# A linear-attention and mixer kernel: batch 0's v cast, its chain of small products, and the order of batch 1's q loads

## The chip, the cores and the metric

The kernel runs on one core of a Trainium2 chip. A core has TensorE (matrix products into PSUM, with a separate weight load ahead of each product), VectorE, ScalarE, GpSimd and SyncE, which run side by side and wait for each other on semaphores, and 16 DMA engines between HBM and the on-chip SBUF. The metric is the time of one execution on the device in microseconds (us), the median of several runs.

## The reference

Attention without softmax, followed by a mixer with a low-rank product along the sequence and a two-layer network along the channels. Eight batches, eight heads, 576 positions, 64 channels a head; all inputs and the output are float32.

```python
theta = np.pi / 2.0 * pos / S
def phi(x, c, s):
    r = np.maximum(x, 0.0)
    return np.concatenate([r * c, r * s], axis=-1)
q_p, k_p = phi(q, cos_w, sin_w), phi(k, cos_w, sin_w)
kv = np.einsum('bhsf,bhsd->bhfd', k_p, v)
z = np.sum(k_p, axis=2)
num = np.einsum('bhsf,bhfd->bhsd', q_p, kv)
den = np.einsum('bhsf,bhf->bhs', q_p, z)[..., None] + 1e-06
attn = num / den
# x = attn, the heads side by side: (batch, 576, 512)
xt = x.transpose(0, 2, 1)
h = xt @ U @ V
u = x + h.transpose(0, 2, 1)
ch = np.maximum(u @ w_ch1, 0.0) @ w_ch2
return u + ch
```

## The kernel before

**Tiling.** The 576 positions are cut in nines: a pair of partitions holds nine consecutive positions, the even partition five and the odd one four. So q, k and v of a batch lie in SBUF as [128 partitions, 8 heads, 5 chunks, 64], chunk 4 (the tail) filled on even partitions alone. `load_odd` (L77) and `load_even` (L71) bring 512 KB and 640 KB for a whole tensor. The staging tiles qst, kst and vst exist once, so a batch's loads wait until the batch before has been read from them.

**Stages of a batch.** Features: VectorE and ScalarE make max(x, 0) times cos and sin of q and k in bf16 (`q_prep`, `k_prep`, L289 and L287). The q features are transposed on TensorE (`qtr_mm`, L368; `qtr_unit`, L356) and copied to SBUF. `kv_unit` (L315) makes kv of four heads, and normally a 65th column of ones in v gives the sum z with it. The x products (q features by kv) are multiplied by the reciprocal of the denominator. A is x by U (`a_mm`, L436); then u transposed is built in PSUM from x (products with the identity, `open_mm`, L935) and A by V (`uTd_mm`, L529). `g1_main` (L541) multiplies by w1 and ScalarE applies relu into `hid`; the second layer follows (`g2_part`, `w_part`).

**Order.** The program is written out by hand. Each engine runs its instructions in the order in which the program names them, and a waiting instruction holds all behind it. SyncE issues the loads of q, k, v; GpSimd issues the loads of U, V, w1 (`w1_load`, four quarters, cast from f32 to bf16 on the way) and w2 (`w2_load`, four quarters). Both use the same 16 DMA engines through two queues. Later batches follow a plan by slots (`attention_plan`), which the change leaves alone.

**Batch 0 is special.** Nothing can hide its attention, so `first_chain` (L942) lays it out step by step. z is summed by products of k features with a column of ones (`z_mm`, L892) into the tile `xz`, a pair of PSUM banks that also takes the denominators and A's sums. Products with a tile of zeros (`keep_warm`, L195) fill TensorE's waits. v is cast by VectorE into `v_ext` (four chunks, 65 columns a head, `v_block`) and its tail by GpSimd into `v_tl` (`v_prep`). The denominators are made for heads 0 to 3 and 4 to 7 apart (`den_mm`, L900), each group with its own reciprocal, and VectorE normalises all ten x blocks (`xh_norm`, L920). Tags such as G3 (three PSUM banks), T1, OA, OB name the banks that a product takes.

**Around the chain.** After the features of k come: the tail of v on GpSimd, w1's four loads (the first between the two tail casts), `first_chain`, the loads of batch 1 in the order q odd, q even, k odd, k even, four of v; then a one-column copy into `mark` on GpSimd that waits for batch 1's v of heads 0 to 3, and w2's four loads behind it. The products with w1 begin with three half blocks of `g1_main`, between which the last two blocks of u transposed are closed (`uTd_close`). Batch 1's q features (`q_prep(1, ...)`, chunk 4 first) come next on VectorE and ScalarE, and their transposes, from slot 1 on, on TensorE. The first product with w2 is at slot 16. SyncE's next loads, batch 2's, stand behind a gate: a two-byte copy that waits for w2's second quarter.

Of the kernel before, what the change touches and what calls it, by code (L numbers as in the profile page):

```python
# [10 lines left out]
FP32 = mybir.dt.float32  # L11
# [6 lines left out]
def kernel(  # L18
# [111 lines left out]
    for h0 in (0, 4):  # L130
        load_odd(vst, v, 0, h0, h0 + 4)
        load_even(vst, v, 0, h0, h0 + 4)
    def load_uv():
        nc.gpsimd.dma_start(out=stV, in_=moe_V)
        nines_u = moe_U.rearrange("(m k) r -> m (k r)", k=9)
        nc.gpsimd.dma_start(
            out=stU[:, 0:4, :].rearrange("p c r -> p (c r)"),
            in_=bass.AP(
                tensor=nines_u.tensor, offset=nines_u.offset,
                ap=[[9 * R, TS], [5 * R, 2], [1, 4 * R]],  # L140
            ),
        )
        for lo in (0, TS):
            nc.gpsimd.dma_start(out=stU[lo : lo + TS, 4, :], in_=nines_u[:, 4 * R : 5 * R])
# [59 lines left out]
    mark = const.tile([TS, 1], FP32)  # L204
    mark2 = const.tile([1, 1], BF16)

    V_nat = const.tile([R, S], BF16)
# [69 lines left out]

    def v_block(b, h0, h1, c0, c1, eng):
        cast(
            eng,  # L280
            v_ext[b % 2][:, c0:c1, h0:h1, 0:D].rearrange("p c h d -> p h c d"),
            vst[:, h0:h1, c0:c1, :],
        )

    def scaled_relu(eng, o, i, w):
# [29 lines left out]
    def kv_unit(b, hg, tag, bufs, eng=None):  # L315
        if b not in kv_sb:
            kv_sb[b] = pool.tile([P, H, E], BF16, tag="kv", bufs=2, name="kv")
        acc = bank([P, 4, E], FP32, tag, bufs, "kv_ps")
        vx = v_ext[b % 2]
        for i in range(4):  # L320
            h = hg * 4 + i
            for c in range(5):
                nc.tensor.matmul(  # L323
                    out=acc[:, i, :],
                    lhsT=k_p[b][:, c, h, :] if c < 4 else k_tl[:, h, :],
                    rhs=v_tl[:, h, :] if c == 4 and b < 2 else vx[:, c, h, :],
                    start=(c == 0),
                    stop=(c == 4),
                )
        cast(eng or V_, kv_sb[b][:, hg * 4 : hg * 4 + 4, :], acc)  # L330

# [588 lines left out]
    def xh_norm(b, c, h0, rec, acc):  # L920
# [6 lines left out]
            in0=acc[rows],  # L927
            in1=rec[rows, c, :].unsqueeze(2).to_broadcast([P if c < 4 else TS, 4, D]),
            op=ALU.mult,
# [5 lines left out]
    def open_mm(b, d, t, cs):  # L935
        for c in cs:
# [3 lines left out]
            )  # L940

    def first_chain(b, xz, v_ps):  # L942
        z = xz[:, 0, 0:H]
        d = [
            xz[:, 0, H + 20 * i : H + 20 * i + 20].rearrange("p (c h) -> p c h", h=4)
            for i in range(2)
        ]
        rec = [pool.tile([P, 5, 4], FP32, tag="rec5", bufs=2, name="rec5") for _ in d]
        for h0 in (0, 4):
            v_block(b, h0, h0 + 4, 0, 4, V_)  # L950
        cast(V_, V_bf, v_ps.rearrange("r (c p) -> r c p", c=4))
        cast(A_, z_sb, z)
        kv_unit(b, 0, *T1, A_)
        den_mm(b, 0, 4, d[0])
        recip(rec[0], d[0])
        x0 = [xh_mm(b, c, 0, *t) for c, t in zip(ORD, (G3, G3, G3, OA, OB))]
        den_mm(b, 4, 8, d[1])
        kv_unit(b, 1, *T1, A_)
        for n in range(2):
            xh_norm(b, ORD[n], 0, rec[0], x0[n])  # L960
        recip(rec[1], d[1])
        for n in range(2, 5):
            xh_norm(b, ORD[n], 0, rec[0], x0[n])
        x1 = [xh_mm(b, c, 4, *t) for c, t in zip(ORD[0:4], (G3, G3, G3, OA))]
        for n in range(2):
            xh_norm(b, ORD[n], 4, rec[1], x1[n])
        uT_alloc(b)
# [4 lines left out]
        for n in range(2, 5):  # L972
            xh_norm(b, ORD[n], 4, rec[1], x1[n])
        for i, (tag, bufs) in enumerate((T1, OB, OA)):
# [162 lines left out]
```

## Time and profile before

| what | value |
|---|---|
| median of 3 runs | 299.06 us (298.85 to 299.60) |
| profiled execution | 298.44 us, span 296.7 us |
| granted TensorE clock over the span | 1.0 |
| VectorE, ScalarE, GpSimd busy | 183.8, 158.1, 73.4 us |
| HBM read and written | 36.86 MB, 9.44 MB |
| transposes of batch 0's q on TensorE | 8.9 to 12.0 us |
| first kv product of batch 0 | 15.83 us |
| second kv eviction on ScalarE | 19.01 us |
| first product with w1 | 22.70 us |
| first transposes of batch 1's q | 25.28 us |
| first product with w2 | 40.28 us |

The profile is of one execution. Its span runs from the first instruction to the last; the rest of the execution's time lies around it. A row of the timeline has a start, a duration, the engine, the line of the program and the tiles that are written and read, and in brackets how long the engine had been idle and what ended that. Matmul rows overlap: a product of 512 columns takes 379 ns and the next starts 216 ns later. Times in this document count from the start of the span.

### The profile page before, as it was taken

Reading aid. Unit: us, or ns where it says so; the run is one execution under the profiler, and the core shown is the slowest. Engines: PE = TensorE matmul, PEld = TensorE weight load, DVE = VectorE, ACT = ScalarE, POOL = GpSimd, SP = SyncE. Lnnn points to the kernel's source line nnn. Section 1 sums busy time; section 2 is a strip of 40 time slices with the busy share of each in tenths; the row PEclk is TensorE's granted clock in tenths of the full one; section 3 lists DMA queues with packets and bytes.
Section 4 is the critical chain, followed back from the end, with each engine's and each line's share of the span. In section 5 each row is a group of like instructions: output and inputs, shape, how many; then the busy total and the mean of one; then the engine's idle time right before and its main releaser. Section 6 shows DMA issues by size and latency. Waiting matters only on the chain.

```text
span 296.7 us, 7055 instructions
## 1 busy us (share of the span) xinstructions
PE 290.1 (98%) x2948; PEld 195.1 (66%) x2948; DVE 183.8 (62%) x359; ACT 158.1 (53%) x269; POOL 73.4 (25%) x113
## 2 busy tenths in 40 slices
PE   8999999999999999999999999999999999999994
PEld 6775455545987547854887547855887547845982
DVE  4898748887884668738734687538734586404341
ACT  2835561476693467745692457746692453067300
POOL 8340500050053305540051500540051101300130
PEclk9999999999999999999999999999999999999999
DMA  7999999999949994999999808996375104030004
GB/s 205 352 273 255 226 186 261 291 232 236 287 82 164 266 357 106 251 241 269 232 163 226 325 2 198 177 310 187 73 129 171 38 2 88 8 136 2 0 15 165
DMA packets 85281, 53.30 MB, mean 180 GB/s; under 512 B 54018, under 2 KB 82978, under 8 KB 85250
## 3 DMA queue, kind: packets, MB, share of 16 engines
q1 hardware_dynamic: 78802, 41.40, 59.0%
q0 software_dynamic: 6368, 11.43, 15.6%
q8 instruction: 23, 0.38, 0.5%
q14 instruction: 8, 0.07, 0.1%
q10 hardware_dynamic: 80, 0.03, 0.0%
HBM read 36.86 MB, written 9.44 MB: 156 GB/s over the span
## 4 chain that ended last, share of the span: by engine, by line
PE 95%; DMA 2%; ACT 1%; DVE 0%; issue 0%; ACTq 0%
PE g_ps L551 38%; PE w_ps L729 29%; PE gt_ps L571 5%; PE o_ps L611 5%; PE ot_ps L638 5%; PE x_ps L413 3%; PE kv_ps L339 2%; DMA qst<-in_q_dram 2%; PE w_ps L198 1%; PE va_ps L464 1%; PE a_ps L439 1%; PE kv_ps L323 1%; PE t_ps L368 1%; PE t_ps L356 1%; PE xh_ps L914 1%; PE va_ps L484 0%
## 5 line engine op out<-in xcount | busy, mean ns | idle before, releaser
L560 ACT ACTIVATE hid<-g_ps 128x512 bf16<-128x512 f32 x128 | 76.1, 597 | 85.1 <-PE g_ps L551 58.4
L551 PE MATMUL g_ps<-uT,w_bf 128*128 128x512 bf16 x512 | 120.8, 379 | 0.0
L551 PEld LDWEIGHTS <-w_bf 128*128 128x128 bf16 x512 | 46.3, 98 | 48.8 <-issue 0.2
L741 POOL TENSOR_TENSOR o_sb<-w_sum,u_bf 128x512 f32<-128x512 f32 x21 | 26.4, 1283 | 124.0 <-DVE w_sum L741 124.0
L729 PEld LDWEIGHTS <-hid 128*128 128x128 bf16 x448 | 43.6, 98 | 5.6
L729 PEld LDWEIGHTS <-S 128*128 128x128 bf16 x336 | 32.6, 98 | 4.1 <-DVE S L697 0.2
L741 DVE TENSOR_TENSOR o_sb<-o_sb,w_ps 128x512 f32<-128x512 f32 x28 | 19.2, 686 | 17.5 <-PE w_ps L729 11.1
L729 PE MATMUL w_ps<-w_bf,hid 128*128 128x256 bf16 x224 | 26.9, 273 | 0.0
L729 PE MATMUL w_ps<-T,hid 128*128 128x256 bf16 x224 | 26.7, 273 | 0.0
L729 PE MATMUL w_ps<-T,S 128*128 128x256 bf16 x224 | 26.0, 273 | 0.0
L473 DVE TENSOR_TENSOR u_bf<-x_bf,va_ps 128x1024 bf16<-128x1024 bf16 x16 | 19.3, 1216 | 7.2 <-PE va_ps L464 7.2
L114 POOL CAST v_ext<-vst 128x512 bf16<-128x512 f32 (+1 forms) x30 | 19.3, 678 | 13.2 <-DMA vst<-in_v_dram 12.8
L423 DVE TENSOR_TENSOR x_bf<-x_ps,rec 128x512 bf16<-128x512 f32 x28 | 19.4, 691 | 1.0
L697 DVE TENSOR_TENSOR S<-hid 128x1024 bf16<-128x1024 bf16 x14 | 9.7, 693 | 15.3 <-ACT hid L560 15.3
L403 DVE TENSOR_SCALAR rec<-x_ps 128x8 f32<-128x8 f32 (+1 forms) x35 | 5.7, 164 | 20.1 <-PE x_ps L413 20.0
L287 ACT ACTIVATE k_p<-kst,sinw 128x512 bf16<-128x512 f32 x26 | 17.1, 712 | 0.2 <-DMA kst<-in_k_dram 0.2
L585 POOL DMA_DIRECT2D out_dram<-o_sb x12 | 7.6, 630 | 38.3 <-DVE o_sb L619 21.4
L114 DVE CAST kv<-kv_ps 128x520 bf16<-128x520 f32 (+1 forms) x8 | 5.1, 632 | 17.5 <-PE kv_ps L339 13.9
L611 PE MATMUL o_ps<-w_bf,hid 128*128 128x512 bf16 x64 | 15.6, 379 | 0.0
L571 PEld LDWEIGHTS <-w_bf 128*128 128x128 bf16 x256 | 14.7, 98 | 0.9
L571 PE MATMUL gt_ps<-uT_tl,w_bf 128*128 128x128 bf16 x256 | 15.3, 219 | 0.0
L638 PE MATMUL ot_ps<-w_bf,hid_tl 128*128 128x512 bf16 (+2 forms) x80 | 15.0, 336 | 0.0
(145 smaller groups left out, 366.2 us busy)
## 6 DMA issues: line engine op xcount, KB each, us to landing
qst<-in_q_dram SPq DMA_DIRECT2D x14, 512.0 KB, 6.2
kst<-in_k_dram SPq DMA_DIRECT2D x14, 512.0 KB, 9.1
vst<-in_v_dram SPq DMA_DIRECT2D x12, 512.0 KB, 8.2
out_dram<-o_sb POOLq DMA_DIRECT2D x12, 512.0 KB, 6.7
w_bf<-in_moe_w_ch_dram POOLq DMA_DIRECT2D x8, 512.0 KB, 10.6
out_dram<-o_sb SPq DMA_DIRECT2D x4, 512.0 KB, 3.0
qst<-in_q_dram SPq DMA_DIRECT2D x2, 640.0 KB, 7.0
kst<-in_k_dram SPq DMA_DIRECT2D x2, 640.0 KB, 10.8
```

The source lines that it names most:

```text
L114: eng.tensor_copy(out=o, in_=i)
L287: nc.scalar.activation(out=o, in_=i, func=AF.Relu, bias=0.0, scale=w)
L423: nc.vector.tensor_tensor(out=x_of(b, c, rows).rearrange("p (g i d) -> p g i d", g=2, d=D), in0=view[:, :, :, 0:D], in1=rec[rows].unsqueez ...
L473: nc.vector.tensor_tensor(out=u_bf[b][:, d0 : d0 + 2], in0=x_bf[b].rearrange("p c (d n) -> p d c n", n=P)[:, d0 : d0 + 2], in1=va_ps[b, d0 ...
L551: nc.tensor.matmul(out=g_ps.rearrange("p (c t) -> p c t", c=4), lhsT=w1_bf[:, d, j * P : j * P + P], rhs=uT[b][:, d, :, :], start=(d == 0) ...
L560: nc.scalar.activation(out=hid[b][:, j, :], in_=g_ps, func=AF.Relu, bias=0.0, scale=1.0)
L571: nc.tensor.matmul(out=g_ps[:, jj, :], lhsT=w1_bf[:, d, j * P : j * P + P], rhs=uT_tl[pr][:, d, :], start=(d == 0), stop=(d == 3),)
L611: nc.tensor.matmul(out=o, lhsT=hid[0][:, j, cc * P : cc * P + P], rhs=w2_bf[:, j, :], start=(j == 0), stop=(j == NJ - 1),)
L638: nc.tensor.matmul(out=o[:, cols], lhsT=hid_tl[pr][:, j, :], rhs=w2_bf[:, j, cols], start=(j == 0), stop=(j == NJ - 1),)
L697: V_.tensor_tensor(out=o, in0=a, in1=b_, op=op)
L729: nc.tensor.matmul(out=res[:, g, :], lhsT=lhs[:, k_, g * P : g * P + P], rhs=rhs[:, k_, :], start=(opens and k_ == 0 and g == 0), stop=(k_ ...
L741: eng.tensor_tensor(out=o, in0=x, in1=y, op=ALU.add)
```

## The change

Five things are done in the first 24 us and in the order around them.

- v of batch 0 is cast by VectorE alone, all five chunks, into a new tile `v0` in the space of `hid`, two heads, two heads and four heads at a time; kv of batch 0 has 64 columns a head. GpSimd's casts of the tail are gone.
- All denominators of batch 0 lie in one row, [5 chunks, 8 heads], with one reciprocal.
- The chain is dealt out anew: the sine of k's tail goes to VectorE; V_bf, one x block (`xh_norm_act`, four activations) and the second eviction of u transposed go to ScalarE; A's second half goes to VectorE, from a bank of its own. Banks and keep-warm products are moved, fills are added, and the spread of V comes ahead of k's last two z groups.
- GpSimd: w1's first load stands behind a one-column copy that waits for v of heads 0 to 3, the other three behind one that waits for ScalarE's first kv eviction.
- SyncE: between the odd and the even rows of batch 1's q stands a four-byte copy into `mark3` that waits for the last v of batch 0.

The three half blocks of `g1_main` follow the two closings together.

```diff
+    v0 = pool.tile([P, H, 5, D], BF16, tag="hid", bufs=1, name="v0")
...
+        n = D if b == 0 else E
+        acc = bank([P, 4, n], FP32, tag, bufs, "kv_ps")
...
+                    rhs=(
+                        v0[:, h, c, :] if b == 0
+                        else v_tl[:, h, :] if c == 4 and b < 2 else vx[:, c, h, :]
+                    ),
...
+    def xh_norm_act(b, c, h0, rec, acc):
+        x_alloc(b)
+        rows = slice(0, P) if c < 4 else tail(b)
+        for i in range(4):
+            nc.scalar.activation(
+                out=x_of(b, c, rows)[:, (h0 + i) * D : (h0 + i) * D + D],
+                in_=acc[rows, i, :], func=AF.Copy, bias=0.0,
+                scale=rec[rows, c, h0 + i : h0 + i + 1],
+            )
...
-        for h0 in (0, 4):
-            v_block(b, h0, h0 + 4, 0, 4, V_)
-        cast(V_, V_bf, v_ps.rearrange("r (c p) -> r c p", c=4))
-        cast(A_, z_sb, z)
-        kv_unit(b, 0, *T1, A_)
-        den_mm(b, 0, 4, d[0])
-        recip(rec[0], d[0])
+        d = xz[:, 0, H : H + 40].rearrange("p (c h) -> p c h", h=H)
+        rec = pool.tile([P, 5, H], FP32, tag="rec5", bufs=1, name="rec5")
+        fill(1)
+        for h in (0, 2):
+            cast(V_, v0[:, h : h + 2], vst[:, h : h + 2])
+        qtr_evac(b, 4, V_, t_q[4])
+        cast(V_, v0[:, 4:H], vst[:, 4:H])
+        cast(A_, z_sb, xz[:, 0, 0:H])
+        kv_unit(b, 0, *G3, A_)
+        cast(A_, V_bf, v_ps.rearrange("r (c p) -> r c p", c=4))
+        den_mm(b, 0, H, d)
+        recip(rec, d)
         x0 = [xh_mm(b, c, 0, *t) for c, t in zip(ORD, (G3, G3, G3, OA, OB))]
-        den_mm(b, 4, 8, d[1])
         kv_unit(b, 1, *T1, A_)
+        fill(2)
+        xh_norm_act(b, ORD[4], 0, rec, x0[4])
+        for n in range(4):
+            xh_norm(b, ORD[n], 0, rec, x0[n])
...
-        uTd_mm(b, 0)
-        uTd_evac(b, 0, A_)
-        uTd_mm(b, 1)
-        uTd_evac(b, 1, V_)
-        a_mm(b, a_ps, (2, 3), range(5))
-        cast(A_, A_of(b)[TS:P, :], a_ps[TS:P, :])
+        for i in range(2):
+            uTd_mm(b, i)
+            uTd_evac(b, i, A_)
+        a2 = bank([P, P], FP32, *G3, "a_ps")
+        a_mm(b, a2, (2, 3), range(5))
+        cast(V_, A_of(b)[TS:P, :], a2[TS:P, :])
...
-    keep_warm(2, *T1)
+    v_ps = None
     for c in TL:
-        k_prep(0, c, (V_, A_))
-        keep_warm(2 if c < 2 else 1, *T1)
+        k_prep(0, c, (V_, A_ if c < 4 else V_))
+        if c < 3:
+            keep_warm((3, 1, 1)[c], *T1)
+        if c == 3:
+            v_ps = spread_v(*T1)
         z_mm(0, c, xz[:, 0, 0:H])
-        if c == 1:
-            qtr_evac(0, 4, V_, t_q[4])
-    v_ps = spread_v(*OB)
     qtr_evac(0, 3, A_, t_q[3])
 
-    v_prep(0, 0, 4, (4,), (G_,))
+    G_.tensor_copy(out=mark, in_=vst[0:TS, 3, 4, 0:1])
     w1_load(0)
-    v_prep(0, 4, 8, (4,), (G_,))
+    first_chain(0, xz, v_ps)
+    G_.tensor_copy(out=mark[0:1], in_=kv_sb[0][0:1, 0, 0:1])
     for n in range(1, 4):
         w1_load(n)
-    first_chain(0, xz, v_ps)
     load_odd(qst, q, 1)
+    nc.sync.dma_start(out=mark3, in_=vst[0:1, 4, 4, 0:1])
     load_even(qst, q, 1)
...
-    g1_main(0, 0, True)
     uTd_close(0, 2, V_)
     uTd_close(0, 3, A_)
-    g1_main(0, 1, True)
-    g1_main(0, 2, True)
+    for j in range(3):
+        g1_main(0, j, True)
```

`fill(n)` makes n products of 384 columns with the tile of zeros into the second bank of `xz`.

More of the change, by code (lines that the diff above doesn't have):

```diff
@@ L205 @@
     mark2 = const.tile([1, 1], BF16)
+    mark3 = const.tile([1, 1], FP32)
     V_nat = const.tile([R, S], BF16)
@@ L317, in kv_unit @@
             kv_sb[b] = pool.tile([P, H, E], BF16, tag="kv", bufs=2, name="kv")
-        acc = bank([P, 4, E], FP32, tag, bufs, "kv_ps")
+        n = D if b == 0 else E
+        acc = bank([P, 4, n], FP32, tag, bufs, "kv_ps")
         vx = v_ext[b % 2]
@@ L329, in kv_unit @@
                 )
-        cast(eng or V_, kv_sb[b][:, hg * 4 : hg * 4 + 4, :], acc)
+        cast(eng or V_, kv_sb[b][:, hg * 4 : hg * 4 + 4, 0:n], acc)
     def kv_pair(b, tag, bufs):
@@ L927, in xh_norm @@
             in0=acc[rows],
-            in1=rec[rows, c, :].unsqueeze(2).to_broadcast([P if c < 4 else TS, 4, D]),
+            in1=rec[rows, c, h0 : h0 + 4].unsqueeze(2).to_broadcast([P if c < 4 else TS, 4, D]),
             op=ALU.mult,
@@ new lines, in first_chain, with fill @@
+    def first_chain(b, xz, v_ps):
+        def fill(n):
+            for _ in range(n):
+                nc.tensor.matmul(
+                    out=xz[:, 1, P:512], lhsT=zero[:, 0:P], rhs=zero[:, 0:384],
+                    start=True, stop=True,
+                )
+        d = xz[:, 0, H : H + 40].rearrange("p (c h) -> p c h", h=H)
[10 more added lines that the diff above has]
+        recip(rec, d)
@@ L956, in first_chain @@
         x0 = [xh_mm(b, c, 0, *t) for c, t in zip(ORD, (G3, G3, G3, OA, OB))]
-        den_mm(b, 4, 8, d[1])
         kv_unit(b, 1, *T1, A_)
-        for n in range(2):
[L960 to L966, printed above, removed]
+        fill(2)
@@ L967, in first_chain @@
+        xh_norm_act(b, ORD[4], 0, rec, x0[4])
+        for n in range(4):
+            xh_norm(b, ORD[n], 0, rec, x0[n])
+        x1 = [xh_mm(b, c, 4, *t) for c, t in zip(ORD[0:4], (G3, G3, G3, T1))]
+        for n in range(2):
+            xh_norm(b, ORD[n], 4, rec, x1[n])
         uT_alloc(b)
@@ L972, in first_chain @@
         for n in range(2, 5):
-            xh_norm(b, ORD[n], 4, rec[1], x1[n])
-        for i, (tag, bufs) in enumerate((T1, OB, OA)):
+            xh_norm(b, ORD[n], 4, rec, x1[n])
+        for i, (tag, bufs) in enumerate((OA, OB, T1)):
             uT_ps[b, i] = bank([P, 4, P], FP32, tag, bufs, "uT_ps")
```

13 lines of the change are left out of this document (removed).

## The prediction

> **What bounds the kernel now.** I read the page first: busy time and the 40 slices.
>
> ```profile
> PE 290.1 (98%) x2948; PEld 195.1 (66%) x2948; DVE 183.8 (62%) x359; ACT 158.1 (53%) x269; POOL 73.4 (25%) x113
> ...
> PE   8999999999999999999999999999999999999994
> ```
>
> TensorE is busy in every slice, so only its holes can be won, or new ones made. The second view, busy time by stretch, says where they are (columns: stretch, its length, busy us of PE, PEld, DVE, ACT, POOL, granted clock, DMA share, GB/s).
>
> ```profile
> 19.00:20.00 1.00, 0.55 (x16) 0.54 (x15) 1.00 (x4) 0.39 (x1) 0.00 (x0) 1.00 1.15 245
> ...
> 22.00:23.00 1.00, 0.74 (x10) 0.41 (x7) 0.26 (x1) 0.40 (x2) 0.00 (x0) 1.00 1.17 249
> ...
> 24.00:33.00 9.00, 9.00 (x79) 5.18 (x78) 8.04 (x16) 5.06 (x10) 0.00 (x0) 1.00 1.17 253
> ```
>
> After 24 us TensorE has no hole to speak of, at full clock; what can be gained lies ahead of that, and from 24 us on any operand that comes late is paid in full. The DMA engines are full throughout. Third, the chain of waits in order of time (start, us, what).
>
> ```profile
> 16.61 0.48 PE xz L903 x20
> 17.09 0.77 PE xh_ps L914 x20
> 17.86 0.48 PE xz L903 x20
> 18.34 0.66 PE kv_ps L323 x20
> 18.99 0.02 issue
> 19.01 0.40 ACT kv L112
> ...
> 22.16 0.28 ACT A_sb L112
> ...
> 22.48 0.38 PE u L937 x4
> ...
> 25.45 0.45 PE t_ps L356 x8
> ...
> 40.44 0.86 PE o_ps L611 x4
> ```
>
> The chain runs through TensorE with two breaks: the second kv eviction (19.01), and A_sb (22.16), which the fourth block of opening products waits for because it shares a bank with A's sums. At 25.28 by the timeline (25.45 in the chain) come the transposes of batch 1's q tail, at 40.28 the first products with w2. Fourth, the transfers, asked for by stretch: queue lines of 24 to 33, then of 42.1 to 46.0, then the issues at 11.00, 13.99 and 33.21 (last column: us from issue to landing).
>
> ```profile
> q0 software_dynamic: 1071, 1.06, 69.6%
> q1 hardware_dynamic: 1068, 1.20, 46.4%
> ...
> q0 software_dynamic: 792, 0.79, 123.0%
> ...
> qst<-in_q_dram SPq DMA_DIRECT2D x1, 640.0 KB, 7.7
> ...
> w_bf<-in_moe_w_ch_dram POOLq DMA_DIRECT2D x1, 512.0 KB, 8.4
> ...
> w_bf<-in_moe_w_ch_dram POOLq DMA_DIRECT2D x1, 512.0 KB, 5.7
> ```
>
> When both queues have work they share packet for packet (1071 to 1068 in 9 us), some 120 to 133 GB/s each as counted; alone, SyncE's queue moved 357 GB/s (13 to 15 us) and GpSimd's 208 (it casts, so it reads twice what is counted). From 42.1 to 46.0 SyncE's queue moved nothing, though the timeline has it issuing at 42.17, 43.05, 43.80 and 44.47: behind a full GpSimd queue a new transfer took 3.0 to 3.8 us to begin. At the start, with nothing else moving, it took 1.5 (issue 0.73, first packets 2.3).
>
> **The chain of batch 0, part by part.** TensorE from the end of the transposes, 12.00, to the first denominator product, 16.45: after the change four keep-warm products (4 x 0.22), a hole of 0.22 as before, five groups of z (0.22 each), two more keep-warm, the spread of V (0.39), one fill (0.16), 20 kv products (0.61): 3.8, to 15.76. That is 0.7 earlier. ScalarE allows it: its fourth sine product of k ends at 14.39 as before, the fourth z group wants it at 14.55, and k_tl's sine has gone to VectorE (0.40, starting 13.8).
>
> VectorE's casts of v start at 14.2. 640 contiguous columns are not in the trace: by the row of 512 (four casts in 1.42 us, 0.355 each) 0.44, by the row of 1024 (two in 1.68) 0.53. I take 0.5: two end by 15.2, and heads 2 and 3 want the second at 15.45. Cover 0.2; cost 0 to 0.1. The cast of four heads (0.9 to 1.05, after q_tlT's 0.6) ends by 16.9, wanted by the second kv unit at 17.5.
>
> Denominators: 40 products in one row (1.0) in place of 20 and 20 (0.5 each): nothing on the sum before the second kv unit, and one reciprocal pair less for VectorE (0.4). V_bf goes to ScalarE (0.60), which was idle from 17.03 to 19.01: hidden, and T's bank is free at 16.7, before the second kv unit. The two fills (0.33) lie in the hole at 18.8. The chunk that ScalarE normalises: four activations of 64 columns, between 0.16 (8 columns) and 0.27 (128 columns) each, 0.65 to 1.1 in all, ending 19.3 to 19.7; TensorE wants it at 19.45: 0 to 0.25, I take 0.1, which VectorE's four norms instead of five give back.
>
> A's second half now has a bank of its own and VectorE evicts it, so the fourth opening block no longer waits: the hole of 0.43 at 22.0 goes. Both uT evictions on ScalarE end at 21.9, when the first g products come. The halves of g1 start at 21.97 and end at 23.27; before, the same point was 24.41. **Gain 1.1**; 0.7 if the hole comes back at the closing products, 1.3 if the first hole goes too. GpSimd loses two casts (0.46, 0.62), off the path. w1's first quarter is issued at 13.7 instead of 13.99 and wanted at 22.0; at its old 8.4 it lands at 22.1, and with SyncE's queue empty beside it earlier: 0.
>
> **What moves in the queues.** On SyncE the small copy mark3 waits for batch 0's last v, issued at 6.22 and landed 8.8 later, 15.0. Behind it stand q's even rows (before: 11.00), k odd, k even and four v transfers. mark3 costs 0.76 like the copy at 42.17, so q even is issued at 15.9. w1's first quarter is in its queue by then, with packets from 16.3 (13.99 took until 16.6). So q even starts behind a running GpSimd queue: at best 1.5 later, 17.4; at worst 3.84, 19.7. I take 3.4, 19.3, because its neighbour says so: k odd, issued at 14.41, moved hardly anything before 18 (79 hardware packets against 246 software ones from 17 to 18.5). From there k odd, 512 KB, took until 23.5, 5.5 us; k even landed 4.5 after it. 640 KB shared: 5.8. **q even lands at 25.1** (23.2 to 25.5); before it was 18.7.
>
> Who waits: VectorE's cosine and ScalarE's sine of q_tl, which the new chain wants at 22.7, then TensorE's transposes of it, reached at 24.13. 25.1 and 0.87 (sine 0.71, hand-overs) make 25.97: **stall 1.84** (0 to 2.25). Chunks 0 to 3 follow at the old spacing.
>
> The Trainium skill's page "DMA: Bandwidth & Descriptors" (section "Latency and other measured facts") gives about 0.6 us to the first byte of a hardware-issued transfer. By it q even would start at 16.5 and land at 22.3, and there would be no stall; the rows above show 1.5 on an empty machine and 3.0 or more on a full one, so they decide, and the rule's result is the first rival.
>
> The same bytes with an idle gap in front (15.2, when q's odd rows are through, to 16.3) and SyncE's queue behind GpSimd's: batch 1's even v for heads 0 to 3, landed 33.0 before, comes at 34.8 to 35.6, and w2's four loads wait for it on GpSimd. 5.7 after issue w2's first quarter lands at 40.6 to 41.5; before it was 38.95. TensorE, shifted by -1.1 + 1.84 = +0.74, wants it at 41.0: 0 to 0.5, I take 0.25. Later things have cover: the last v, 1.2 late at 37.3, is cast by 39.4 and used at 41; batch 2's loads, behind w2's second quarter on SyncE, 1.7 late, feed ScalarE at 50.5 to 51.9, whose next product for TensorE is at 53.9. w1's other quarters, behind ScalarE's kv eviction on GpSimd (16.3 instead of 15.64), queue behind the first anyway.
>
> **Sum**, against the profiled execution's 298.44 (span 296.7 and 1.74 around it): 298.44 - 1.1 + 1.84 + 0.25 = 299.43, which is +1.0. The median of the runs is 299.06, 0.62 above that execution; on it 300.0.
>
> **Rivals.** First, the gate is harmless: q even starts at 17.4 or earlier, lands by 23.3, w2 by 39.2, and the chain's 1.1 stays: 298.0. For it: the idle start's 1.5 us, and one GpSimd transfer only just begun. Against it: k odd's slow beginning.
> Second, gain and stall cancel: start near 18.4, landing 24.2, stall 0.95, w2 in time: 298.9. For it: 18.4 lies between the two measured delays, 2.5 after the issue.
> Third, SyncE's queue is held until GpSimd's is drained, as 42.1 to 46.0 can be read too (w2's last load landed at 48.0): 2.1 MB of w1 at 208 GB/s from 16.3 end at 26.4, q even 2.8 later at 29.2 (0.66 MB at 357, and 1.0 to land), stall 5.9: 303.9. Against it: the even sharing from 18.5 on. It decides if no hardware packet is seen while w1 runs.
>
> **How the numbers follow.** About 0.3%, 0.9 us, is what a measurement of this kernel can tell from no change. Forecast, a stall that outweighs the gain: 0.42; gate harmless 0.24; cancelling 0.26; held 0.08. Slower is the first and last, 0.50; within 0.3% 0.26; faster 0.24. The range goes from the full gain at its upper bound, 297.8, to the smallest gain with the longest stall, -0.7 + 2.25 = +1.55 or 300.6, and 1.2 more for what lands late behind it (the lateness of the last v, if its cover fails): 301.8. The forecast's own range is 299.4 to 300.9.
>
> **What would show it.** Right: TensorE's first g products near 22.0, a hole of 1 to 2 us ahead of the q_tl transposes, VectorE and ScalarE there waiting for q's transfer, and a hole or none at 41 before the first w2 product. Wrong: q's even rows landed before 23.4; the first g products after 22.5; a hole at the second kv unit, which would mean that the casts of v are slow.

## The result, and the profile after

| what | before | after |
|---|---|---|
| median, 20 runs of each | 298.89 us (298.40 to 300.51) | 301.84 us (297.82 to 303.78) |
| ratio | | 1.0056, 95% interval 1.0029 to 1.0083 |
| profiled execution, span | 298.44, 296.7 us | 299.02, 297.1 us |
| first kv product of batch 0 | 15.83 | 14.64 |
| first product with w1 | 22.70 | 22.46 |
| first transposes of batch 1's q | 25.28 | 24.63 |
| first product with w2 | 40.28 | 41.00 |

The change makes the kernel slower, by 0.6% as the ratio has it. The ratio is one of means and leaves out the five runs of the changed kernel that lie over 1.5% above its fastest, so it is smaller than that of the two medians. The changed kernel's runs spread over 6 us, those of the kernel before over 2; the one that was profiled is among its shortest, and it shows only a part of what the change costs. The page of that execution (busy time, then the slices):

```profile
PE 289.1 (97%) x2916; PEld 195.7 (66%) x2947; DVE 183.3 (62%) x357; ACT 159.3 (54%) x273; POOL 72.7 (24%) x113
...
PE   8999989999999999999999999999999999999994
...
PEclk9979999999999999999999999999999999999999
```

The third digit of the last line is new: over the slice from 14.9 to 22.3 us the granted clock is 0.77 on average, because it is half from 16.49 to 19.90. The same stretches as before, in busy time by stretch (columns as there):

```profile
19.00:20.00 1.00, 1.00 (x24) 0.91 (x23) 0.77 (x3) 0.58 (x3) 0.00 (x0) 0.55 0.99 337
22.00:23.00 1.00, 1.00 (x9) 0.43 (x7) 0.44 (x1) 0.79 (x2) 0.00 (x0) 1.00 1.16 245
24.00:33.00 9.00, 8.95 (x78) 5.11 (x77) 7.30 (x14) 4.77 (x9) 0.00 (x0) 1.00 1.17 253
```

The holes of the first two stretches (0.55 and 0.74 us busy before) are gone, yet the clock in the first is 0.55: TensorE is busy there in part because its products take longer. In the third nothing is missing, so in this execution batch 1's q was not late. The chain of waits:

```profile
14.80 0.58 PE kv_ps L320 x20
15.38 0.99 PE xz L903 x40
...
18.00 16.50 DMA vst<-in_v_dram
...
34.62 0.18 POOL mark L1043
...
35.08 5.89 DMA w_bf<-in_moe_w_ch_dram
...
41.00 1.02 PE o_ps L611 x4
```

The 40 denominator products take the expected 1.0, kv comes a little over 1 us earlier, and what ends last is no longer TensorE: batch 1's v landed at 34.50 (33.03 before), the mark behind it let w2's first quarter start at 35.08, and that landed at 40.96, 2.0 later than before. TensorE stood 1.11 us for it. (A hole is counted here from the time at which the next product could have started, 216 ns after the start of the last; the idle times in the views count from that product's end and are 0.16 shorter.) The transfers by stretch: 16.17 to 17.62, 17.62 to 20.59 and 24 to 33, then the issue of q's even rows (15.11, last column: us to landing).

```profile
q0 software_dynamic: 287, 0.29, 122.4%
q1 hardware_dynamic: 2, 0.00, 0.3%
...
q1 hardware_dynamic: 693, 0.82, 87.9%
q0 software_dynamic: 68, 0.05, 11.7%
...
q0 software_dynamic: 1073, 1.07, 69.7%
q1 hardware_dynamic: 1074, 1.19, 46.2%
...
qst<-in_q_dram SPq DMA_DIRECT2D x1, 640.0 KB, 6.5
```

For 1.45 us SyncE's queue got nothing beside w1. Then, in this execution, w1's first quarter was through (19.05) and the second sent no packet before 20.59, so q's even rows had the engines almost alone and landed at 21.57. For q this is the rival that the prediction called harmless gate; for w2 it is not, since that rival had w2 by 39.2. Nor is it the usual course: in the four other profiles with mark3 q landed at 25.7 to 26.2.

Where every microsecond lies can be read from five times of a profile. The table gives, for each profiled execution of this study, the start of the first transposes of batch 0's q, then the us from there to the first w1 product, from there to the transposes of batch 1's q, from there to the first w2 product, and from there to the end (the execution's time less the sum of the others). In brackets are TensorE's holes above 0.5 us in that stretch that end with a transfer's landing, directly or by one operation behind it.

| kernel | first | to w1 | to q_tl | to w2 | rest | time |
|---|---|---|---|---|---|---|
| before | 8.89 | 13.81 | 2.58 | 15.00 | 258.16 | 298.44 |
| after | 8.62 | 13.84 | 2.17 | 16.37 (1.11) | 258.02 | 299.02 |
| e1_no_mark3 | 9.19 | 13.75 (1.05) | 2.17 | 14.99 | 258.10 | 298.20 |
| e2_warm | 8.28 | 13.46 | 5.36 (3.19) | 16.13 (1.13) | 258.01 | 301.24 |
| e3_before_mark3 | 8.83 | 13.80 | 4.31 (1.73) | 15.30 | 258.03 | 300.27 |
| e4_after_again | 8.45 | 13.20 | 5.27 (3.10) | 16.31 (1.30) | 258.05 | 301.28 |
| e5_no_mark3_warm | 8.26 | 15.24 (1.88) | 2.17 | 14.99 | 258.07 | 298.73 |
| e6_w1_after_k | 8.33 | 14.07 (0.62) | 2.17 | 15.02 | 258.08 | 297.67 |
| e7_before_less_warm | 8.43 | 15.62 | 2.37 | 14.99 | 258.52 | 299.93 |
| e8_no_mark3_again | 8.17 | 16.78 (3.68) | 3.86 | 14.99 | 258.09 | 301.89 |
| e9_w1_split | 8.27 | 13.47 | 2.92 (0.74) | 15.59 (0.59) | 258.08 | 298.33 |
| e10_w1_split_less_warm | 8.63 | 14.18 | 2.33 | 15.51 (0.51) | 258.18 | 298.83 |
| e11_w2_after_k | 8.20 | 13.22 | 5.12 (2.95) | 15.00 | 258.01 | 299.55 |
| e12_k_behind_w1 | 8.07 | 13.81 | 2.17 | 15.08 | 258.16 | 297.29 |

The last stretch is the same to 0.2 us in all but one: everything is decided before 44 us. The first column, 8.07 to 9.19, is taken as chance (no edit here touches what stands ahead of it), so profiled times are compared by the other columns. The 0.62 of e6_w1_after_k is not ahead of w1: it lies at 12.92, where the products for z waited for k of batch 0, which came late in that execution.

### The profile page after: what moved, and what is told of

Read it like the earlier page. It is cut to its first block, busy times and chain, and to the rows that moved or that the text cites. A ratio compares the mean times of both kernels' runs of the same rounds, so it can differ in the third digit from the quotient of the medians.

```text
span 297.1 us, 7024 instructions
## 1 busy us (share of the span) xinstructions
PE 289.1 (97%) x2916; PEld 195.7 (66%) x2947; DVE 183.3 (62%) x357; ACT 159.3 (54%) x273; POOL 72.7 (24%) x113
## 4 chain that ended last, share of the span: by engine, by line
PE 89%; DMA 8%; issue 1%; DVE 1%; SPq 0%; POOL 0%; DVEq 0%; POOLq 0%
PE g_ps L551 33%; PE w_ps L729 29%; DMA vst<-in_v_dram 6%; PE gt_ps L571 5%; PE o_ps L611 5%; PE ot_ps L638 5%; PE w_ps L200 3%; PE x_ps L413 3%; PE kv_ps L339 2%; DMA w_bf<-in_moe_w_ch_dram 2%; PE a_ps L439 1%; PE va_ps L464 1%; PE t_ps L368 1%; PE kv_ps L320 1%; PE va_ps L484 0%
## 5 line engine op out<-in xcount | busy, mean ns | idle before, releaser
L473 DVE TENSOR_TENSOR u_bf<-x_bf,va_ps 128x1024 bf16<-128x1024 bf16 x16 | 19.3, 1217 | 7.2 <-PE va_ps L464 7.2
L114 POOL CAST v_ext<-vst 128x512 bf16<-128x512 f32 (+1 forms) x30 | 18.7, 659 | 12.6 <-DMA vst<-in_v_dram 11.5
L413 PEld LDWEIGHTS <-q_pT 128*128 128x128 bf16 x224 | 10.8, 98 | 5.9
```

Source lines behind the costliest of these rows:

```text
L114: eng.tensor_copy(out=o, in_=i)
L413: nc.tensor.matmul(out=acc[:, g, i * E : i * E + E], lhsT=qT_of(b, c, h), rhs=kv_sb[b][:, h, :], start=True, stop=True,)
L473: nc.vector.tensor_tensor(out=u_bf[b][:, d0 : d0 + 2], in0=x_bf[b].rearrange("p c (d n) -> p d c n", n=P)[:, d0 : d0 + 2], in1=va_ps[b, d0 ...
```

## Experiments

### The copy taken out, the keep-warm put back, the copy alone, and the kernel again

The theory after the result had two parts that had to be told apart: transfers (mark3 makes q's even rows late, and w2 behind them) and the clock (the new chain streams too few columns, and TensorE's clock halves). Four kernels went together; the first two edit the changed kernel, the third the kernel before, the fourth is the changed kernel without an edit.

```diff
e1_no_mark3
-    nc.sync.dma_start(out=mark3, in_=vst[0:1, 4, 4, 0:1])
e2_warm
-            keep_warm((3, 1, 1)[c], *T1)
+            keep_warm((3, 3, 2)[c], *T1)
e3_before_mark3 (before, between load_odd(qst, q, 1) and load_even(qst, q, 1))
+    nc.sync.dma_start(out=mark3, in_=vst[0:1, 4, 4, 0:1])
```

> The changed kernel without the copy into mark3: batch 1's even q rows are issued right after the odd ones, at about 10.4 us, as before the change. Queue theory (SyncE's transfers fall behind GpSimd's, so batch 1's v, and with it w2, comes late): v of heads 0 to 3 lands near 33 again, w2's first quarter near 39, no hole ahead of the first w2 product, median 298.0 to 298.5 and runs close together. Clock theory (too few columns stream through TensorE between 12 and 19 us, so the clock is halved for one window of 3.4 us in many runs): the halved windows stay, the median falls by 1 us at most, to some 300.5 to 301.5, and the runs stay as far apart as they are (297.8 to 303.8).

> The changed kernel with three more keep-warm products of 512 columns among z's groups (3, 3, 2 in place of 3, 1, 1): 0.65 us more on the chain. Clock theory: no window at half clock in the profile between 12 and 20 us, the granted clock of every run at 0.995 or above, the median falls by 1 to 2 us in spite of the 0.65. Queue theory: the hole ahead of the first w2 product only shrinks by what the chain is later, the median stays at 301 to 302.

> The kernel before with nothing but the copy into mark3 between batch 1's odd and even q rows. Queue theory: v of heads 0 to 3 lands 1.5 to 2.5 us later than 33.0, w2's first quarter at 40.6 to 41.5 or later, a hole of 0.5 to 2 us ahead of the first w2 product, median 299.5 to 301.5. Clock theory: as before the change, 298.9 within 0.5, no half clock.

> The changed kernel unaltered, for a second profile and times beside the others on the same chip. Both theories: a median of 300.5 to 302.5, single runs from 298 to 303. Clock theory: the slower of its runs have the lower granted clock, and the profile shows a half-clock window whose place differs from that of the first (16.5 to 19.9). Queue theory: w2's first quarter lands after 40.5 and TensorE has a hole there of 1 us or more, clock or no clock.

| kernel | median (range), runs | ratio (95% interval) |
|---|---|---|
| e1_no_mark3 | 299.86 (297.92 to 302.17), 10 | 1.0038 (1.0002 to 1.0073) |
| e2_warm | 301.49 (301.14 to 302.31), 4 | 1.0085 (1.0064 to 1.0105) |
| e3_before_mark3 | 300.28 (300.19 to 300.33), 4 | 1.0040 (1.0025 to 1.0055) |
| e4_after_again | 300.88 (300.32 to 302.67), 5 | 1.0064 (1.0029 to 1.0098) |

e4_after_again, at 301.28 us, is nearer to the usual execution of the changed kernel. Its waits from 23 to 45 us (us in total, times, longest):

```profile
ACT q_tl L283 <- DMA qst<-in_q_dram: 3.8, 1, 3.8
...
PE t_ps L356 <- ACT q_tl L283: 2.9, 1, 2.9
...
PE o_ps L611 <- DMA w_bf<-in_moe_w_ch_dram: 1.1, 1, 1.1
```

Its transfers from 16.5 to 19.5, from 19.6 to 24, and the issue of q's even rows at 16.66:

```profile
q0 software_dynamic: 517, 0.52, 113.3%
q1 hardware_dynamic: 2, 0.00, 0.1%
...
q0 software_dynamic: 444, 0.45, 69.6%
q1 hardware_dynamic: 394, 0.50, 39.2%
...
qst<-in_q_dram SPq DMA_DIRECT2D x1, 640.0 KB, 9.4
```

And its stretch from 24 to 33:

```profile
24.00:33.00 9.00, 6.08 (x58) 3.90 (x58) 6.66 (x14) 4.08 (x7) 0.00 (x0) 1.00 1.16 254
```

For 3 us behind the issue SyncE's queue moved two packets to GpSimd's 517; then they share, q lands at 26.06, ScalarE's sine of q_tl waits for it and TensorE waits for the sine: 2.9 us out of 9 are gone, at full clock; the half-clock stretch that was expected in this profile is not there. Without the hole e4 takes 13.20 + 2.17 from the first transposes to q_tl's, against 16.39 before: the chain is 1.02 us shorter, and 3.10 + 1.30 is paid for it.

e3_before_mark3 shows the copy by itself, without the new chain. Its waits from 23 us on, and its transfers from 16.09 to 18.98, behind the issue at 15.43:

```profile
ACT q_tl L288 <- DMA qst<-in_q_dram: 2.0, 1, 2.0
```

```profile
q0 software_dynamic: 474, 0.47, 106.9%
q1 hardware_dynamic: 4, 0.00, 0.2%
```

The same gap, the same landing (26.08), a stall of 1.73. It is smaller than in e4 because TensorE arrives later. Of the 0.5 to 2 us that were expected ahead of the first w2 product 0.3 are there (15.30 against 15.00): w2's first quarter landed at 42.20, and TensorE, delayed by q, came to it late itself. The copy costs 1.44 us on the medians (300.28 against 298.84 for the kernel before beside it) with no clock to be seen in it: of the four runs, the two at a mean granted clock of 0.994 took 300.19 and 300.33, the two at 0.997 and 1.0 300.27 and 300.30.

e2_warm speaks against the clock as the main cause: with the keep-warm products back, the clock is 0.997 to 0.999 in three of four runs, and the time is no shorter than e4's, where 1 to 2 us less was expected. Its chain to w1 is 0.26 longer than e4's, its stalls are the same.

e1_no_mark3 was expected to show the gain of the chain, and did so in half its runs: 297.92 to 298.96 in five, 300.77 to 302.17 in the other five. Something else is late there, which the profiled run (one of the first five) shows only as 1.05 us ahead of the first w1 product.

### Without the copy: what splits the runs

e5_no_mark3_warm asks whether the upper group is the clock, by the keep-warm products of e2_warm without mark3; e8_no_mark3_again is e1 unaltered, for a profile of the upper group. e7_before_less_warm tests the clock by itself: the kernel before with four keep-warm products fewer beside k's features. e6_w1_after_k is e5 with w1's first load let go by k instead of v.

```diff
e6_w1_after_k (and e5's two edits: no mark3, keep_warm 3, 3, 2)
-    G_.tensor_copy(out=mark, in_=vst[0:TS, 3, 4, 0:1])
+    G_.tensor_copy(out=mark, in_=kst[0:TS, 3, 4, 0:1])
     w1_load(0)
e7_before_less_warm (before)
-        keep_warm(2 if c < 2 else 1, *T1)
+        if c < 3:
+            keep_warm(1, *T1)
```

> Without the copy into mark3 and with the three more keep-warm products (3, 3, 2). Without mark3 alone the runs fell in two groups, 297.9 to 299.0 and 300.8 to 302.2. Clock theory: the upper group is made of runs in which a window of 3.4 us around 13 to 20 us is at half clock; with three more products of 512 columns the emptiest window is as full as before the change (0.42 of TensorE's columns), and the upper group is gone: all runs 298.0 to 299.3, median 298.5, since the 0.65 us of products lies in the wait for w1's first quarter. Queue theory alone: without mark3 nothing is late but w1's first quarter, so it has no reason for two groups; if they stay, the clock theory falls and something else in the queues makes them.

> The kernel of the run without mark3 and with more keep-warm products, and w1's first load stands behind k's even rows (landed 11.0 to 11.7) instead of v of heads 0 to 3 (12.6 to 13.4). Queue theory: w1's first quarter is issued 1.5 us earlier and lands 1 to 2 us before 22.9, the hole of 1.0 us ahead of the first w1 product goes, the last v lands up to 1 us later since it shares with w1, and the median is 297.6 to 298.3. If v is held up by more than the cover of the second cast (0.2 us for heads 0 to 3), the kv products wait and the median stays at 298.3 to 299. Clock theory: as the other, one group of runs.

> The kernel before with four keep-warm products fewer among z's groups (one each for the first three in place of 2, 2, 1, 1, 1), nothing else. Clock theory: two groups of runs appear, the upper one 1.5 to 3 us above the lower one and with a granted clock of 0.994 or less; the lower one at 298.2 to 298.9, as the chain is up to 0.86 shorter and then waits for w1's first quarter. Queue theory: the queues are those of the kernel before, so one group, 298.2 to 299.0.

> The changed kernel without mark3 once more, for a profile that may fall in the upper group of its runs (300.8 to 302.2). Clock theory: if this run is above 300, its profile shows a half-clock window between 12 and 24 us and slower products in it; if it is below 299, none. Queue theory: a run above 300 shows a transfer that lands late and a hole where it is wanted, at full clock.

| kernel | median (range), runs | ratio (95% interval) |
|---|---|---|
| e5_no_mark3_warm | 300.00 (297.85 to 302.26), 12 | 1.0036 (1.0002 to 1.0071) |
| e6_w1_after_k | 298.58 (297.67 to 300.38), 12 | 0.9989 (0.9964 to 1.0013) |
| e7_before_less_warm | 300.96 (298.49 to 304.76), 10 | 1.0050 (1.0017 to 1.0084) |
| e8_no_mark3_again | 299.88 (298.07 to 303.39), 8 | 1.0016 (0.9983 to 1.0049) |

The two groups stay in e5 (six runs from 297.85 to 299.40, six from 300.59 to 302.26), one run of the upper group at a clock of 1.0. Five of the upper six do stand at 0.991 to 0.993, so the clock goes with the split, and that one run shows that it isn't needed for it. e8's profile is of the upper group, and says what it is. Its waits from 18 to 32 us, then busy time from 21 to 25 and from 25.1 to 28.6:

```profile
PEld L551 <- DMA w_bf<-in_moe_w_ch_dram: 3.8, 1, 3.8
PE g_ps L551 <- DMA w_bf<-in_moe_w_ch_dram: 3.5, 1, 3.5
```

```profile
21.00:25.00 4.00, 0.49 (x6) 0.15 (x4) 2.67 (x6) 1.42 (x3) 0.00 (x0) 1.00 1.17 250
25.10:28.60 3.50, 3.28 (x9) 1.22 (x9) 0.00 (x0) 0.16 (x1) 0.00 (x0) 0.51 1.17 251
```

Without mark3, q's even rows and k's share the engines with w1's first quarter, which landed at 24.91 where the chain wanted it at about 21.3. TensorE stood 3.68 us, and behind that idle its clock was half for 3.41 us more, in which TensorE did nine products where 216 ns each would have let it do sixteen. So q's rows and w1's first quarter are both wanted near 22 us, and the order of the queues decides which is late: with mark3 q, in most executions, and without it w1.

e6 follows from it: w1's packets begin at 16.31 instead of 17.91 (e5), the hole ahead of w1 is gone from the profile, and the median falls by 1.4 to that of the kernel before. It stays above the 297.6 to 298.3 that was expected.

e7 shows that the clock alone can make a kernel slower, with the queues of the kernel before: its runs are at 0.980 to 0.989 in eight of ten runs and at 1.0 only in the shortest (298.49). Its profiled execution, busy time from 18.3 to 21.7 and from 14.9 to 18.3:

```profile
18.30:21.70 3.40, 2.93 (x54) 2.53 (x51) 3.18 (x11) 0.49 (x2) 0.43 (x1) 0.50 1.17 252
14.90:18.30 3.40, 2.89 (x85) 2.50 (x85) 2.19 (x6) 0.97 (x3) 2.30 (x4) 1.00 1.12 312
```

TensorE counts as busy for 85% of the second stretch, but mostly with products of one and of 64 or 65 columns; the half clock comes right behind it. TensorE was at no time idle for more than 0.6 us here. By the table it came to w1 1.81 us later than in the kernel before, without a hole that ends with a transfer.

### w1 in two pieces, w2's mark, and the copy in another place

With the cause known, three kernels take the late operands one by one. Each block of w1 products reads 128 of w1's columns, so the first two blocks need only half of the first quarter, and that can come in two pieces (e9). e10 takes two keep-warm products out of e9. e11 leaves the changed kernel as it is, mark3 included, and lets only w2 go earlier.

```diff
e9_w1_split (e6 and)
-    w1_load(0)
+    w1_load(0, 0, 256)
+    w1_load(0, 256, 512)
...
e10_w1_split_less_warm (e9 and)
-            keep_warm((3, 3, 2)[c], *T1)
+            keep_warm((3, 2, 1)[c], *T1)
e11_w2_after_k (the changed kernel and, ahead of w2's loads)
-    G_.tensor_copy(out=mark, in_=vst[0:TS, 3, 4, 0:1])
+    G_.tensor_copy(out=mark, in_=kst[0:TS, 3, 4, 0:1])
```

> This is the kernel of e6_w1_after_k (no mark3, keep-warm products 3, 3, 2, w1's first mark waiting for k's even rows in place of v) with w1's first quarter loaded in two pieces of 256 columns, 256 KB each. In e6 the quarter landed at 22.28 us and was wanted at about that time, and single runs lay between 297.67 and 300.38 us. Queue theory (what spreads the runs without mark3 is how late w1's first quarter lands, because GpSimd's and SyncE's queues share the DMA engines packet for packet): nothing lands sooner as a whole, but if the products wait by piece, the first piece, with packets from 16.3 at half the engines, lands near 20, so the first half block starts at 21.5 to 22.2 whatever the second piece does until 22.8 or so; the median falls to 297.4 to 298.3 and the spread shrinks to under 2 us. If one semaphore covers both pieces it stays as e6, 298.0 to 299.2. Clock theory (the spread of runs is TensorE's clock halving on too few streamed columns): the split changes nothing, 298.0 to 299.2, with the same spread as e6.

> e9_w1_split with two keep-warm products fewer (3, 2, 1). Clock theory: each product is 0.22 us of the chain, so the chain is 0.44 us earlier where the clock stays whole, median 0.4 below e9; but the streamed columns per 3.4 us fall towards the share at which the changed kernel's profile showed half clock, and in single runs 0.5 to 2 us is lost, the granted clock of those runs being below 0.99. Queue theory: with w1's first quarter the late operand, an earlier chain waits longer for it and the median stays within 0.3 us of e9 with all clocks at 0.997 or above.

> The changed kernel, mark3 and all, with one edit: the mark ahead of w2's loads waits for batch 1's k in place of its v of heads 0 to 3. In e4_after_again (the changed kernel, 301.28 us profiled) k's even rows of batch 1 landed some 4 us ahead of v, w2's first quarter was issued at 37.36 and landed at 43.18, and TensorE stood 1.30 us ahead of the first product with w2, besides 3.10 us ahead of the transposes of batch 1's q. Queue theory: w2's first quarter is issued at 33 to 35 and lands 1 to 4 us earlier, the hole of 1.1 to 1.3 ahead of the first w2 product is gone, the one of 1.5 to 3.1 ahead of q's transposes stays; v lands later, sharing with w2, and could be late for the plan's v casts near 39 us by up to 0.5. Median 299.6 to 300.8, against 301.84 in the 20 runs of the changed kernel. Rival (the wait for w2 is only how an earlier delay shows, cover behind it takes it back): the hole goes, the median stays at 300.9 to 301.8.

| kernel | median (range), runs | ratio (95% interval) |
|---|---|---|
| e9_w1_split | 298.72 (298.29 to 299.68), 11 | 0.9997 (0.9983 to 1.0011) |
| e10_w1_split_less_warm | 298.79 (298.38 to 299.39), 11 | 0.9991 (0.9971 to 1.0011) |
| e11_w2_after_k | 299.66 (297.86 to 302.35), 12 | 1.0018 (0.9998 to 1.0039) |

e9 did half of what was expected. The spread fell from 2.7 to 1.4 us and the first piece landed at 20.24, ahead of the first w1 product at 21.74; but the median did not fall against e6's (297.4 to 298.3 was expected). Its waits of TensorE from 15 to 45 us:

```profile
PE g_ps L551 <- DMA w_bf<-in_moe_w_ch_dram: 1.0, 2, 0.6
```

The second piece (landed 23.31) and w1's second quarter (27.84) are late instead, by 0.74 and 0.59 us at the products' starts. The load that moved beside them is k's, behind q, so it was taken to be in the way; e12 below tests that.

In e10 both theories saw a part: five of eleven runs lie at a clock of 0.993 or 0.994, one of eleven in e9. In the profiled one the clock was half from 16.50 to 19.92, and the stretch to w1 is 0.71 longer than e9's although its two keep-warm products less are worth 0.44. The second piece, wanted later, then costs no hole, so the median is the same: in that execution a wait took up what the clock lost. That the clock falls below 0.99, as the expectation has it, did not happen.

e11 isolates the second cost. w2's hole is gone (15.00 from q_tl to w2, as before), and what is left is q's:

```profile
16.34 9.33 DMA qst<-in_q_dram
...
25.76 0.73 ACT q_tl L283
...
26.54 0.62 PE t_ps L356 x8
```

The chain of waits from 20 us on begins with q's even rows. The median is 1.2 below e4's five runs and 2.2 below the changed kernel's 20, but the intervals of the ratios overlap. The profiles are clearer: from q_tl to w2 it is 1.31 shorter than e4, and the rest is as long (258.01 and 258.05), so cover behind w2 does not take it back and the rival falls. The expectation is wrong in one figure: in e4 k's even rows landed at 35.22, 1.57 ahead of v and not some 4; w2's first quarter was issued at 35.26 and landed at 41.04.

The last kernel puts the copy where these say it belongs: q goes straight through, and it is k's odd rows that wait, for w1's first piece (mark3 is a bf16 tile there). w2's mark waits for k as well, so what each of the two is worth is not shown apart.

```diff
e12_k_behind_w1 (e9 and)
     load_even(qst, q, 1)
+    nc.sync.dma_start(out=mark3, in_=w1_bf[0:1, 3, 255:256])
     load_odd(kst, k, 1)
...
-    G_.tensor_copy(out=mark, in_=vst[0:TS, 3, 4, 0:1])
+    G_.tensor_copy(out=mark, in_=kst[0:TS, 3, 4, 0:1])
     for n in range(4):
         w2_load(n)
```

> e9_w1_split with the copy ahead of a load put where the queue theory wants it: q's even rows go straight behind the odd ones, and it is k's odd rows that wait, until the first piece of w1's first quarter has landed (20.24 us in e9); w2's mark waits for k, as in e11. In e9 the second piece landed at 23.31 and w1's second quarter at 27.84, and TensorE had holes of 0.74 us (22.39) and 0.59 us (27.24) for them; k's features of batch 1 begin at 35.3 there though k had landed at 28.2, so k has 7 us to give. Queue theory: k's odd rows are issued near 21 and begin 3 to 4 us later, so w1 has the engines to itself meanwhile; the second piece lands by 22.6 and the second quarter by 26.5, both holes shrink to 0.3 or less, k's even rows land near 33, w2's first quarter is issued then and lands near 40, about when it is wanted. Profiled time 297.2 to 297.8, median 297.4 to 298.2, below both kernels. Rival (there is too little room in the queues: k or w2 is late instead): a hole of 1 us or more ahead of the first w2 product, or k's features after 36.5, and the median stays at 298.5 to 299.5.

297.53 us median (297.12 to 298.77, 12 runs) against 298.88 for the kernel before beside it, ratio 0.9951 (0.9928 to 0.9974): 0.5% faster than the kernel before, and below the changed kernel's 301.84. Busy time from 22 to 33 us:

```profile
22.00:23.00 1.00, 0.95 (x5) 0.42 (x5) 1.00 (x3) 0.99 (x2) 0.00 (x0) 1.00 1.24 210
24.00:33.00 9.00, 8.95 (x84) 5.07 (x84) 6.72 (x12) 4.83 (x10) 0.18 (x1) 1.00 1.13 299
```

And the end of the chain of waits there:

```profile
35.37 3.83 PE g_ps L551 x17
39.20 0.95 PE o_ps L611 x4
```

From 12 us to the first w2 product no transfer is on the chain, and TensorE waits for none; k's even rows land at 32.67, ahead of their first use at 34.2, and w2's first quarter at 39.09, just in time. The two runs at a clock of 0.994 are its longest (298.67 and 298.77; the ten others 297.12 to 297.81): here, where no wait can take it up, the lower clock, as one half-clock stretch gives it, goes with 1.2 us more.

## Why the prediction was right, and where its sizes were off

**The chain, 1.1 expected.** Right: 1.02 in e4 (15.37 against 16.39 from the first transposes to q_tl's, transfer holes taken out) and 1.00 in e11. In the profiled execution of the changed kernel it is 0.38, since the clock was half for part of it. VectorE's casts of two heads took 476 to 485 ns (0.5 taken), the one of four heads 811 to 828 (0.9 to 1.05 taken), ScalarE's four norms 309 to 334 each, 0.92 in all (0.65 to 1.1 taken). The hole ahead of the fourth opening block is gone.

**q's even rows.** The start was taken as 19.3 within 17.4 and 19.7, and came within it: 17.62 in the profiled execution, 17.89 in e2, 18.98 in e3, 19.47 in e11, 19.57 in e4. That is partly luck, for the rule behind it was wrong. The delay of 3.4 was read from k's odd rows, but these stood behind q's even rows in the same queue, which landed only at 18.67 (of the 79 packets from 17 to 18.5, 36 have the 1280 bytes of q's even rows). And no fixed delay fits: from issue to first packet it was 1.44 us in e2 and 3.55 in e3. What fits is the end of w1's first quarter, as the last section shows. The figure of 0.6 us to the first byte, from the Trainium skill's page "DMA: Bandwidth & Descriptors" (section "Latency and other measured facts"), does not describe a transfer issued while GpSimd's queue is at work: 1.4 to 3.6 us here. The landing was mis-sized: 25.1 was taken, with the bound at 25.5, and it was 25.68 to 26.24 in e2, e3, e4 and e11. From the first packet it took 6.2 to 8.4 us there, where 5.8 had been worked out from k's rows.

**The stall, 1.84 expected.** This is the term of the sum that failed: 3.10, 3.19 and 2.95 in e4, e2 and e11. In e4 three quarters of the difference is q's landing; the rest is that TensorE was there at 23.6 to 23.9 instead of 24.13, since the first transposes came up to 0.7 earlier by chance. An operand that lands at a fixed time turns every gain ahead of it into stall.

**w2, 0.25 expected.** Mis-sized too: 1.11 to 1.30. v was taken to land at 34.8 to 35.6 and w2's first quarter at 40.6 to 41.5. In e4 they came at 36.79 and 43.18. In the profiled execution they came at 34.50 and 40.96, but TensorE was there at 39.89 and not at 41.0, because no stall for q had delayed it. Later things had cover, as the prediction said: the last column of the table does not move.

**w1's first quarter, 0 expected.** Right for the kernel as it is (landed at 19.05, 20.16 and, in e11, 20.33; wanted at 21.4 or later). e1 and e8 show what mark3 bought with it: without it the quarter is 1.05 to 3.68 us late. The prediction had seen only that the copy delays q, not that it keeps the engines free for w1.

**The clock.** Not foreseen: "at full clock" was read from the kernel before and carried over, though the change takes keep-warm products and columns out of the chain. The mean over the span needs care: after TensorE's last product the clock goes half for the last 0 to 2.2 us of every profile, which alone makes means of 0.996 to 1.0; a stretch of 3.41 us at half clock takes off another 0.006, so that 0.994 or less stands for at least one. Of the 20 runs, the eight at a mean clock of 0.997 or more have a median of 300.1, the twelve at 0.994 or less 302.2. How much of those 2.1 us is the clock's own and how much is that a late run idles TensorE and so loses the clock (as in e8) stays open; e12's two runs put one such stretch at 1.2 where nothing takes it up, and e3's at nothing.

**The sum, +1.0 expected.** By the ratio it is +1.7 (0.56% of 298.9), by the medians +2.95. Sign and mechanism were right: a stall ahead of q's transposes that outweighs the gain, and a second wait at the first w2 product. The median, 301.84, is just past the upper end given. **The rivals:** the harmless gate happens in single executions, as far as q goes (the profiled one; of the shortest, 297.82, there is no profile). SyncE's queue held until GpSimd's is drained is half right: q's even rows were held until w1's first quarter was almost through, but not for the other three; in e4 the two queues share from 19.6 on (394 packets to 444).

## What to carry to other kernels

A chain that was made shorter in front of a saturated DMA queue gained nothing here until the operands behind it landed in time, so list for each the time at which it is wanted and the bytes that stand before it; the order that won here delays the load with slack (k, 7 us), not the one that is wanted next (q). A one-element copy that gates a queue costs the wait for its source and, behind a busy second queue, 1.4 to 3.6 us more before the first packet here, so it belongs ahead of a load that can afford that. One profile of a kernel whose runs spread over 6 us need not be of a usual run: take several, and compare them by stretches that end in the same event.

## What the runs showed of the hardware

**The start behind a busy queue.** On the empty machine SyncE's first packets came 1.5 us after issue. q's even rows, issued in the five profiles with mark3 while packets of w1's first quarter were moving, took 1.44 us (e2), 2.51 (after), 2.91 (e4), 3.13 (e11) and 3.55 (e3). What ended the wait can be read from the packets: each quarter of w1 closes with sixteen packets of 4 bytes, and the first of these went out at 17.55, 17.61, 19.10, 19.05 and 18.27 in those profiles, q's first packet 0.34, 0.01, 0.47, 0.42 and 0.71 us behind it. In the kernel before, SyncE's transfers issued from 42.17 on sent their first packet at 46.02, the time of the first closing packet of w2's last quarter; the third quarter's, from 43.47 on, had let nothing through. In the 13 other profiles the two times there are at most 0.13 us apart. So a late transfer waits for GpSimd transfers ahead of it to run out, and not for a fixed time. w1's other quarters, issued at most 0.13 us ahead of q's even rows or behind them, did not hold q; how long ahead a transfer must be issued to hold another is not shown. Once begun, the two queues share packet for packet (1073 to 1074 from 24 to 33 us). How late q landed was then a race: when w1's second quarter sent its first packet, 491 of q's 512 packets were out in the profiled execution (landed 21.57), 448 in e2 (26.24), and none in e3, e4 and e11.

**Half clock with TensorE busy.** The granted clock falls to half for 3.41 us at a time. It did so behind idle time (e8), but also in after, e7 and e10, where TensorE counted as busy for 85 to 100% of the time before. What those have in common is few columns. A product of 512 columns lets the next start 216 ns later, 0.42 ns a column; the columns that started in a stretch, times that, give a share of it. Where the stretch begins can be read too: in each of the 14 profiles the clock changes only at whole multiples of 3.413 us from its first full-clock time (after: 6.25, then 16.49, 19.90 and 296.38, which are 3, 4 and 85 steps). The steps right ahead of the four half-clock ones have shares of 0.41 (after), 0.35 (e7), 0.34 (e10) and 0.06 (e8). Up to TensorE's last product, every other step of every profile has 0.44 or more, but for one of 0.38 (e7, from 11.5), behind which the clock stayed full; so the measure sorts all steps but that one. It also shows why one kernel does both: e4's emptiest 3.41 us have 0.34 like the changed kernel's first profile, but its steps cut them in two, of 0.49 and 0.56. The Trainium skill's page "TensorE: Matmul & The Clock Gate" (section "HAM oscillation — how this bites in real kernels") gives the rule that gaps without work above about 3.4 us are to be avoided; e8's hole of 3.68 us agrees with it, and after, e7 and e10 show that it isn't enough.
